# Moving the layout transfers of q and k to later places in a four-batch attention and mixer kernel

## The chip, the cores and the metric

The kernel runs on one core of a Trainium2 chip. Its time is device microseconds (us) of one launch; for each kernel three executions are shown by their median and their ends. One more execution was profiled, and every row below is from that one.

## The reference

Batch 4, 8 heads, 768 positions, head width 64. The attention works in chunks of 32 queries; each chunk sees 8 memory keys, the 16 positions before it, its own 32 and the 8 after it. Its result x then goes through a low-rank token mix and a two-layer network:

```python
for c in range(24):
    k_full = concat([mem_k, k[l_start:r_end]]); v_full = concat([mem_v, v[l_start:r_end]])
    a = softmax(q_c @ k_full.T / 8)
    out[c] = a @ v_full
x = out.transpose(0, 2, 1, 3).reshape(4, 768, 512)
u = x + ((x.transpose(0, 2, 1) @ U) @ V).transpose(0, 2, 1)     # U 768x32, V 32x768
y = u + relu(u @ w_ch1) @ w_ch2                                  # 512 -> 2048 -> 512
```

U, V, w_ch1 and w_ch2 arrive as float64; q, k, v and the memory as float32.

## The kernel before

**Arithmetic.** The float64 weights are decoded on the device; each becomes a high and a low half (`w1h`, `w1l`, cast on ACT at L387, subtracted on DVE at L391), and each product of the network is made in three passes of 128-row matmuls. DRAM scratch (`w1s`, `w1x`) keeps low halves and sums of weights for the later batches.

**Order of the batches.** Batch 0 runs its attention, then 32 *units* (`both_blocks`). A unit is one hidden group f of 128 columns for one half of the 768 positions: `w1_step` (12 matmuls at L1475), a split into `hh` (ACT) and `hl` (DVE), and `w2_step` for the unit before. The first 20 units decode the weights as they go; units 20 to 25 are f = 10 to 15 of the first half, units 26 to 31 of the second. The attention of batch 1 is a Python generator, and a table, `PLACE`, says after which matmuls of units 18 to 31 it is advanced by how many pieces.

Batches 1 to 3 (`sevens`) make pairs of hidden groups with seven products of sums (`six`, L1302), with weights that a ring (`wlo`, four items ahead) brings from the scratch (L1261, L465 to L468). Batch 1 differs: its first part makes ten single hidden groups f = 0 to 9 (`half_of`, `other`), with sums of weights made on ACT and DVE (L488, L489) and stored to the scratch (L494). While batch b runs, the attention of batch b + 1 is advanced by `give()`, which spreads 49 pieces evenly over a batch's places. The *second part* of a batch is the loop over n = 0 to 15, which only needs kept hidden groups.

**Layout of q and k.** For batches 0 and 1, q and k are loaded as rows (`kraw`, L539 to L549), regrouped (`kn`; POOL at L567 for batch 1), turned by TensorE (L618) and copied by ACT into `kall` (L655 to L659) and `qt` (L679). For batches 2 and 3 a DRAM-to-DRAM transfer first rearranges them: `spread(b)` issues eight transfers on SP's queue, four for k and then four for q, each of 3072 rows of 128 bytes (L172). Then `load_blocks` (L526) reads 256 KB at a time and DVE transposes blocks of 32x32 into `kall` (L637, two instructions per load) and `qt` (L668, one). The table `SPREAD` says in which unit of batch 0 a spread is issued: one in each of units 2 to 17.

**What sets the order.** PE and SP keep the order in which the program is written. From unit 27 on (and on ACT and POOL after the first units) a scheduler orders ACT, DVE and POOL by priority. SP issues almost all DMAs, in order: an issue that must wait for its data holds back all behind it.

```python
for n, (blk, f, where, begins, ends) in enumerate(units):
    ...
    for _ in range(SPREAD.get(n, 0)):
        next(spreading)
    ...
    hid_ = w1_step(0, blk, f, w1l, between if n else joins)
```

Of the kernel before, what the change touches and what calls it, by code (L numbers as in the profile page):

```python
# [48 lines left out]
LATER = 4  # L49
NPIECE = 49  # L50
DIRECT = 2
SPREAD = {n: 1 for n in range(2, 18)}
PLACE = {
# [7 lines left out]
def chunk_attn_then_mixer_kernel(  # L61
# [454 lines left out]
    def attention(b, xs):  # L516
# [114 lines left out]
        def k_blocks(T, h):  # L631
            raw, p = kn.pop((T, h)), slice(2 * h, 2 * h + 2)
            kt = kall[:, NB * (T % 2):NB * (T % 2) + NB, p]
            other = kall[:, NB * ((T + 1) % 2) + NB - 1, p]
            at, own = NM + LEFT, NM + LEFT + CK
            for q_ in range(2):
                nc.vector.transpose(out=kt[:, :, q_, at:own], in_=raw[:, q_])  # L637
            nc.scalar.copy(out=kt[:, 1:, :, NM:at], in_=kt[:, 0:NB - 1, :, own - LEFT:own])
            nc.scalar.copy(out=kt[:, 0:NB - 1, :, own:], in_=kt[:, 1:, :, at:at + NW - own])
            if T > 0:  # L640
                nc.scalar.copy(out=kt[:, 0, :, NM:at], in_=other[:, :, own - LEFT:own])
                nc.scalar.copy(out=other[:, :, own:], in_=kt[:, 0, :, at:at + NW - own])
# [648 lines left out]
    def sevens(b, give, following, last_step=None):  # L1291
# [45 lines left out]
        if few:  # L1337
            banks, lows = {}, {}

            def half_of(f):  # L1340
                banks[f], lows[f] = hidden_bank(), next_item()
                six(banks[f], w1h[f][:, 0:2], lows[f][:, 0], 0, True)
                keep(kept(f), banks[f])

            def other(f):
                low = lows.pop(f)
                six(banks[f], w1h[f][:, 2:4], low[:, 1], 1, False)
                if f < few - 2:
                    take_value(f, low.rearrange("p i c n -> p (i c) n"), work_home)
                return split(banks.pop(f)[:, :TOK])  # L1350

            last_step()
            half_of(0)
            half_of(1)
            for _ in gen[0]:
                pass
            gen[0] = attention(b + 1, xs)
            prev = (0, 0, True, None) + other(0)
            for f in range(1, few):
                h = other(f)  # L1360
                if f == 1:
                    send()
                if f + 3 == few:
                    plain.close()
                    su1 = ctx.enter_context(tc.tile_pool(name="su1", bufs=1, reuse_waits="tile"))
                    hst.append(su1.tile([P, 4, TOK], F32, name="hst2"))
                    seven["pools"] = su1, []
                if f + 1 == few:
                    closing.enter_context(tc.manual_schedule(engines=CLOSING))
                early, late = NEXTS.get(few - f, (0, 0))  # L1370
                for _ in range(early):
                    next(coming[0])
                give()
                if f + 1 < few:
                    half_of(f + 1)
                w2_step(b, 0, *prev, give)
                for _ in range(late):
                    next(coming[0])
                if f + 2 == few:
                    save_sums()  # L1380
                prev = (f, 0, False, None) + h
            held_w.close()
            seven["pools"][1].append(ctx.enter_context(tc.tile_pool(name="su2", bufs=1, side="right", reuse_waits="tile")))
# [63 lines left out]
        for n, f in enumerate(order):  # L1447
            hid_ = split(kept(f))
            if n == 0:
                rows.pop()  # L1450
            if n == 2:
                save_sums()
                send()
            if n == LATER and following is not None:
                following()
            give()
            if n + 2 < few:
                other_half(left[n + 2])
                if n < LATER:
                    give()  # L1460
            if prev is not None:
                w2_step(b, 1, *prev)
            prev = (f, 0, n == 0, True if n == NF - 1 else None) + hid_
# [159 lines left out]
    front[0] = False  # L1623
    wide[0] = None

    gen, coming = [None], [iter(())]

    def pace(slots):
        tried, given = [0], [0]

        def give():
            tried[0] += 1
            if tried[0] > slots:
                next(coming[0], None)
                return
            while given[0] < NPIECE * tried[0] // slots:
                next(gen[0], None)
                given[0] += 1

        return give  # L1640
# [12 lines left out]
    last_step = both_blocks()  # L1653
    for b in range(1, B):
        slots = 2 * 2 * NPL - 1 + 6 * (NF // 2 - NPL) + 2 + 2 * LATER if b == 1 else 6 * (NF // 2) + LATER
        if b > 1:
            gen[0] = attention(b + 1, xs) if b + 1 < B else iter(())
            coming[0] = seven_u(b + 1) if b + 1 < B else iter(())
        sevens(b, pace(slots), following_batch(b) if b + 1 < B else None, last_step)
        for _ in coming[0]:  # L1660
            pass
    manual.close()
# [29 lines left out]
```

## Time and profile before

| | |
|---|---|
| three executions: median (ends) | 667.92 us (666.58 to 668.73) |
| the profiled execution: time / span | 667.71 us / 665.8 us |
| PE busy | 629.6 us, 95% of the span |
| DVE / ACT / POOL busy | 365.4 / 236.1 / 77.5 us |
| DMA | 115.02 MB in 168704 packets, of them 100956 under 512 B |

PE is TensorE's matmuls, PEld its weight loads; the two overlap. A time in brackets at the end of a row of the timeline is the idle time of that engine just before, with what ended it. SPq is SP's queue of DMA issues. PEclk is the granted TensorE clock as a share of full speed (1.00 is 2.4 GHz, 0.50 is 1.2 GHz). In this execution batch 0's attention lasts to about 55 us, its units to about 232 us, batch 1 to 388 us, batch 2 to 537 us.

### The profile page before, as it was taken

How to read it: one execution, taken by the hardware profiler on the slowest of the kernel's cores; microseconds unless marked ns; L12 is line 12 of the kernel's file. 1: busy time of each engine (PE TensorE's matmuls, PEld its weight loads, DVE VectorE, ACT ScalarE, POOL GpSimd, SP SyncE). 2: the span in 40 equal slices, each digit the busy share in tenths (PEclk: the TensorE clock that was granted, in tenths of full speed). 3: DMA queues.
4: the chain of work that ended last, by engine and by line, in shares of the span. 5: the costliest groups of instructions: out<-in, count | busy, mean ns of one | idle time of the engine just before them, and what ended most of it. 6: DMA issues, size and time to landing. Idle time of an engine off the chain costs nothing.

```text
span 665.8 us, 14969 instructions
## 1 busy us (share of the span) xinstructions
PE 629.6 (95%) x6078; PEld 544.2 (82%) x6078; DVE 365.4 (55%) x715; ACT 236.1 (35%) x557; POOL 77.5 (12%) x106
## 2 busy tenths in 40 slices
PE   7688999986899999999999999999999999999997
PEld 4547999975687788889879888889988899999886
DVE  5947788893667556953734744434536732222322
ACT  4525435344533445532312622413224512121221
POOL 5100000004136546200400000000000000000000
PEclk9989999997999999999999999999999999999999
DMA  8796999999477279766573059685523046555301
GB/s 233 152 322 214 237 226 241 230 241 300 116 137 214 96 268 264 260 171 155 167 233 104 28 166 264 205 230 136 159 64 126 1 129 190 157 156 161 109 1 47
DMA packets 168704, 115.02 MB, mean 173 GB/s; under 512 B 100956, under 2 KB 139484, under 8 KB 168636
## 3 DMA queue, kind: packets, MB, share of 16 engines
q1 hardware_dynamic: 168012, 113.92, 61.3%
q8 instruction: 48, 0.79, 0.5%
q10 hardware_dynamic: 624, 0.15, 0.1%
q14 instruction: 20, 0.16, 0.1%
HBM read 90.83 MB, written 28.97 MB: 180 GB/s over the span
## 4 chain that ended last, share of the span: by engine, by line
PE 59%; DVE 4%; DMA 4%; SPq 3%; issue 1%; ACT 1%; POOL 1%; ACTq 0%
PE ps_h L1302 23%; PE acc L1526 17%; PE acc L1536 9%; DMA blocks<-spread 3%; PE ps_a L773 2%; PE acc L1520 2%; PE ps_h L1475 2%; PE ps_a L699 1%; SPq L600 1%; PE ps_a L1198 1%; DMA w1l<-w1s 1%; PE ps_a L803 1%; PE ps_a L753 1%; DVE x L1491 1%; PE ps_a L1103 1%
## 5 line engine op out<-in xcount | busy, mean ns | idle before, releaser
L1526 PE MATMUL acc<-w,hh 128*128 128x512 f32 x612 | 158.5, 395 | 0.6 <-ACT hh L1316 0.6
L1526 PEld LDWEIGHTS acc<-w,hh 128*128 128x128 f32 x612 | 112.9, 188 | 20.7 <-ACT hh L1316 0.9
L1536 PE MATMUL acc<-w,hl 128*128 128x512 f32 x306 | 87.9, 396 | 0.0
L1536 PEld LDWEIGHTS acc<-w,hl 128*128 128x128 f32 x306 | 57.3, 189 | 11.9
L1302 PE MATMUL ps_h<-t12h,w1l 128*128 128x384 f32 x192 | 56.3, 345 | 2.0 <-DMA w1l<-w1s 1.4
L1302 PE MATMUL ps_h<-bh,w1l 128*128 128x384 f32 x192 | 52.9, 340 | 0.0
L1302 PE MATMUL ps_h<-t34h,w1l 128*128 128x384 f32 x152 | 46.5, 347 | 1.0 <-issue 0.8
L1475 PE MATMUL ps_h<-uh,w1h 128*128 128x384 f32 x124 | 43.0, 350 | 2.2 <-ACT w1h L387 1.2
L1475 PE MATMUL ps_h<-ul,w1h 128*128 128x384 f32 x124 | 41.6, 339 | 0.4 <-DVE ul L1180 0.4
L1302 PEld LDWEIGHTS ps_h<-t12h,w1l 128*128 128x128 f32 x192 | 35.3, 188 | 5.3 <-ACT hh L1316 2.5
L1317 DVE SCALAR_TENSOR_TENSOR hl<-ps_h,hh 128x384 fp32r<-128x384 f32 x29 | 16.1, 555 | 42.8 <-ACT hh L1316 42.7
L1324 DVE TENSOR_TENSOR c<-ps_h,c 128x384 f32<-128x384 f32 x19 | 10.5, 553 | 50.2 <-PE ps_h L1302 50.2
L1316 ACT ACTIVATE hh<-hst 128x384 fp32r<-128x384 f32 x36 | 18.9, 525 | 49.9 <-PE acc L1526 44.6
L1317 DVE SCALAR_TENSOR_TENSOR hl<-hst,hh 128x384 fp32r<-128x384 f32 x36 | 20.1, 557 | 29.0 <-PE acc L1536 28.5
L1302 PEld LDWEIGHTS ps_h<-bh,w1l 128*128 128x128 f32 x192 | 35.1, 188 | 0.8
L1302 PE MATMUL ps_h<-b,w1l 128*128 128x384 f32 x174 | 35.4, 339 | 0.1
L1324 DVE TENSOR_TENSOR hst<-ps_h,hst 128x384 f32<-128x384 f32 x36 | 19.9, 553 | 24.4 <-ACT hst L1328 15.3
L1302 PE MATMUL ps_h<-t12l,w1l 128*128 128x384 f32 x96 | 32.4, 338 | 0.0
L1316 ACT ACTIVATE hh<-ps_h 128x384 fp32r<-128x384 f32 x29 | 14.2, 490 | 49.1 <-PE ps_h L1302 49.0
L1302 PEld LDWEIGHTS ps_h<-b,w1l 128*128 128x128 f32 x174 | 30.9, 188 | 0.5 <-DVE hst L1324 0.5
L1302 PEld LDWEIGHTS ps_h<-t34h,w1l 128*128 128x128 f32 x152 | 28.0, 188 | 3.1 <-issue 1.7
L1328 ACT COPY c<-ps_h 128x384 f32<-128x384 f32 x19 | 9.1, 479 | 59.5 <-PE ps_h L1302 59.5
(250 smaller groups left out, 1201.9 us busy)
## 6 DMA issues: line engine op xcount, KB each, us to landing
w1l<-w1s SPq DMA_DIRECT2D x155, 256.0 KB
rw<-in_moe_w_ch_dram SPq DMA_DIRECT2D x14, 512.0 KB
out_dram<-x SPq DMA_DIRECT2D x24, 256.0 KB
blocks<-spread SPq DMA_DIRECT2D x24, 256.0 KB
vb<-in_v_dram SPq DMA_DIRECT2D x56, 98.0 KB
raw<-in_moe_w_ch_dram SPq DMA_DIRECT2D x20, 256.0 KB
rw<-in_moe_w_ch_dram SPq DMA_DIRECT2D x16, 256.0 KB
w1s<-sums SPq DMA_DIRECT2D x16, 256.0 KB
```

What stands on the lines that cost most here:

```text
L600: nc.sync.dma_start(out=vt[r0:r0 + NW - NM, n0:n1, D * j:D * j + D], in_=bass.AP(rows.tensor, rows.offset, [[step, count], [CK * step, n1 ...
L699: nc.tensor.matmul(out=psv[s][(slice(CK * i, CK * i + CK), t) + ((p // 2, p % 2) if b >= DIRECT else (p % 2, p // 2))], lhsT=qt[p // 2][ro ...
L773: nc.tensor.matmul(out=psv[g][CK * i:CK * i + CK, t, j], lhsT=pt[s][rows, 2 * t + k_, CK * i:CK * i + CK], rhs=vt[rows, NI * t + i, D * j: ...
L1302: nc.tensor.matmul(out=ps[:, :TOK], lhsT=w_, rhs=u, start=(start and m == 0), stop=(m == 5), skip_group_check=True,)
L1316: nc.scalar.activation(out=hh, in_=c, func=AF.Relu)
L1317: nc.vector.scalar_tensor_tensor(out=hl, in0=c, scalar=0.0, in1=hh.bitcast(F32), op0=ALU.max, op1=ALU.subtract,)
L1324: nc.vector.tensor_tensor(out=out, in0=ps[:, :TOK], in1=in1, op=ALU.add)
L1328: nc.scalar.copy(out=out, in_=ps[:, :TOK])
L1475: nc.tensor.matmul(out=ph[:, :TOK], lhsT=w[:, c, :], rhs=u[c], start=(m == 0), stop=(m + 1 == len(parts)),)
L1520: nc.tensor.matmul(out=acc[tt], lhsT=h[:, sl], rhs=w, start=False, stop=(m == 2))
L1526: nc.tensor.matmul(out=acc[tt], lhsT=h[:, sl], rhs=w, start=(begins and m == 0), stop=False,)
L1536: nc.tensor.matmul(out=acc[tt], lhsT=hl[:, sl], rhs=w2h[f], start=False, stop=ends is not None)
```

## The change

The 16 spreads leave units 2 to 17. Batch 2's four k spreads go to units 22 to 25. Two of its q spreads go right behind batch 0's last step, at the start of batch 1, and two more into batch 1's step f = 1, just ahead of the loads of batch 2's first blocks. Batch 3's eight spreads go one each to n = 4 to 11 of batch 1's second part. There, at n = 12 and 14, the generator of batch 3's attention is also advanced by two pieces each time: the memory values and the four block loads of its first third are then issued before batch 2 starts; `pace` starts batch 2 with those 4 pieces counted as given, so that the later ones keep their places. In `k_blocks` one DVE transpose of 128x512 elements takes the place of two of 128x256.

```diff
--- before.py
+++ after.py
@@ -49,7 +49,7 @@
 LATER = 4
 NPIECE = 49
 DIRECT = 2
-SPREAD = {n: 1 for n in range(2, 18)}
+SPREAD = {22: 1, 23: 1, 24: 1, 25: 1}
 PLACE = {
     18: [0, 0, 0, 1], 19: [0, 0, 0, 2], 20: [0, 0, 0, 3], 21: [3, 3, 4, 5], 22: [6, 7, 9, 11], 23: [12, 13, 14, 15],
     24: [15, 15, 16, 17], 25: [18, 18, 19, 20], 26: [20, 20, 21, 22], 27: [22, 23, 24, 24], 28: [25, 25, 26, 26],
@@ -633,8 +633,7 @@
             kt = kall[:, NB * (T % 2):NB * (T % 2) + NB, p]
             other = kall[:, NB * ((T + 1) % 2) + NB - 1, p]
             at, own = NM + LEFT, NM + LEFT + CK
-            for q_ in range(2):
-                nc.vector.transpose(out=kt[:, :, q_, at:own], in_=raw[:, q_])
+            nc.vector.transpose(out=kt[:, :, :, at:own].rearrange("c i p n -> c p i n"), in_=raw)
             nc.scalar.copy(out=kt[:, 1:, :, NM:at], in_=kt[:, 0:NB - 1, :, own - LEFT:own])
             nc.scalar.copy(out=kt[:, 0:NB - 1, :, own:], in_=kt[:, 1:, :, at:at + NW - own])
             if T > 0:
@@ -1350,6 +1349,8 @@
                 return split(banks.pop(f)[:, :TOK])
 
             last_step()
+            for _ in range(2):
+                next(spreading)
             half_of(0)
             half_of(1)
             for _ in gen[0]:
@@ -1367,6 +1368,9 @@
                     seven["pools"] = su1, []
                 if f + 1 == few:
                     closing.enter_context(tc.manual_schedule(engines=CLOSING))
+                if f == 1:
+                    for _ in range(2):
+                        next(spreading)
                 early, late = NEXTS.get(few - f, (0, 0))
                 for _ in range(early):
                     next(coming[0])
@@ -1451,8 +1455,13 @@
             if n == 2:
                 save_sums()
                 send()
+            if few and LATER <= n < LATER + 8:
+                next(spreading)
             if n == LATER and following is not None:
                 following()
+            if few and n in (LATER + 8, LATER + 10):
+                for _ in range(2):
+                    next(upcoming[0])
             give()
             if n + 2 < few:
                 other_half(left[n + 2])
@@ -1623,10 +1632,10 @@
     front[0] = False
     wide[0] = None
 
-    gen, coming = [None], [iter(())]
-
-    def pace(slots):
-        tried, given = [0], [0]
+    gen, coming, upcoming = [None], [iter(())], [None]
+
+    def pace(slots, ahead):
+        tried, given = [0], [ahead]
 
         def give():
             tried[0] += 1
@@ -1653,10 +1662,12 @@
     last_step = both_blocks()
     for b in range(1, B):
         slots = 2 * 2 * NPL - 1 + 6 * (NF // 2 - NPL) + 2 + 2 * LATER if b == 1 else 6 * (NF // 2) + LATER
-        if b > 1:
-            gen[0] = attention(b + 1, xs) if b + 1 < B else iter(())
+        if b == 1:
+            upcoming[0] = attention(3, xs)
+        else:
+            gen[0] = upcoming[0] if b + 1 < B else iter(())
             coming[0] = seven_u(b + 1) if b + 1 < B else iter(())
-        sevens(b, pace(slots), following_batch(b) if b + 1 < B else None, last_step)
+        sevens(b, pace(slots, 4 if b == 2 else 0), following_batch(b) if b + 1 < B else None, last_step)
         for _ in coming[0]:
             pass
     manual.close()
```

Lines move by -1 up to about L1340, then by +9 to +11 (L1475 becomes L1484, L1317 becomes L1316). PE's order does not change. Three other places do.

First, SP's queue at batch 1's first loads of k (`kraw`), in unit 17 before. These are the rows before, with the last spread of the sixteen, and then the rows now.

```order
L334 DMA rw_1752<-in_moe_w_ch_dram 128x2x256
L334 DMA raw<-in_moe_w_ch_dram 128x2x256
L351 DMA raw<-in_moe_w_ch_dram 128x512 x2
L172 DMA spread_1634<-in_q_dram 3072x1x32
L366 DMA w1s_131<-w1h_1741 128x2x256
L366 DMA w1s_131<-w1l 128x2x256
L539 DMA kraw<-in_k_dram 120x4x128
L540 DMA kraw<-in_k_dram 8x4x128
```

```order
L334 DMA rw_1733<-in_moe_w_ch_dram 128x2x256
L334 DMA raw<-in_moe_w_ch_dram 128x2x256
L351 DMA raw<-in_moe_w_ch_dram 128x512 x2
L366 DMA w1s_131<-w1h_1722 128x2x256
L366 DMA w1s_131<-w1l 128x2x256
L539 DMA kraw<-in_k_dram 120x4x128
L540 DMA kraw<-in_k_dram 8x4x128
```

The spread ahead of `kraw` is gone, as are the fifteen further up the queue; the first one now stands behind all `kraw` and `qraw` loads of batch 1.

Second, ACT during batch 1's turning of q and k: copies out of PSUM into `kall` and `qt`, between casts of the last weights (L387) and decoding steps (L230). Before:

```order
L659 COPY kall<-ps_a 128x2x2x12
L679 COPY qt<-ps_a 128x2x128 x4
L655 COPY kall<-ps_a 128x2x8x16
L656 COPY kall<-ps_a 128x2x7x12
L655 COPY kall<-ps_a 128x2x8x16
L656 COPY kall<-ps_a 128x2x7x12
L659 COPY kall<-ps_a 128x2x2x12
L387 CAST w1h_2065<-vb_115 128x512
L387 CAST w2last<-vb_115 128x512
L230 ACTIVATE vb_115<-rw_1752 128x256
L230 ACTIVATE vb_115<-raw 128x256 x3
L679 COPY qt<-ps_a 128x2x128 x4
```

and now:

```order
L678 COPY qt<-ps_a 128x2x128 x4
L654 COPY kall<-ps_a 128x2x8x16
L655 COPY kall<-ps_a 128x2x7x12
L654 COPY kall<-ps_a 128x2x8x16
L655 COPY kall<-ps_a 128x2x7x12
L658 COPY kall<-ps_a 128x2x2x12
...
L658 COPY kall<-ps_a 128x2x2x12
L678 COPY qt<-ps_a 128x2x128 x2
L387 CAST w1h_2047<-vb_115 128x512
L387 CAST w2last<-vb_115 128x512
L230 ACTIVATE vb_115<-rw_1733 128x256
L678 COPY qt<-ps_a 128x2x128 x2
L230 ACTIVATE vb_115<-raw 128x256 x3
```

The first four `qt` copies now stand ahead of both groups of five `kall` copies, and two of the last four ahead of the casts and the decoding.

Third, SP's queue in batch 1's steps f = 0 and 1, where batch 2's first blocks are loaded (`mv` are memory values, `w1l` ring items, `w1s` stores). Before:

```order
L494 DMA w1s_132<-vb_115 128x512 x2
L494 DMA w1s_132<-sums 128x512 x2
L1501 DMA out_dram<-x 128x512 x3
L956 DMA mv<-in_mem_v_dram 8x4x64 x2
L526 DMA blocks<-spread_1121 128x2x256
L468 DMA w1l<-w1s_129 128x2x256
L526 DMA blocks<-spread_1121 128x2x256
L526 DMA blocks<-spread_1293 128x2x256
```

and now:

```order
L494 DMA w1s_132<-vb_115 128x512 x2
L494 DMA w1s_132<-sums 128x512 x2
L1510 DMA out_dram<-x 128x512 x3
L172 DMA spread_3101<-in_q_dram 3072x1x32 x2
L955 DMA mv<-in_mem_v_dram 8x4x64 x2
L526 DMA blocks<-spread_2011 128x2x256
L468 DMA w1l<-w1s_129 128x2x256
L526 DMA blocks<-spread_2011 128x2x256
L526 DMA blocks<-spread_3101 128x2x256
```

Two spreads of q now stand ahead of all block loads, and the load from `spread_3101` reads what they write.

## Rows read from the trace of the kernel before

**Rows 1.** The page's first part: busy time of each engine, share of the span, instructions.

```profile
PE 629.6 (95%) x6078; PEld 544.2 (82%) x6078; DVE 365.4 (55%) x715; ACT 236.1 (35%) x557; POOL 77.5 (12%) x106
```

**Rows 2.** Timeline of PE, 146 to 184 us: start, length, instruction, idle before.

```profile
154.61 1.11 PE L618 MATMUL ps_a<-ident,kn 128*128 128x128 f32 x4 [7.32 <-POOL kn L567]
...
164.35 0.63 PE L618 MATMUL ps_a<-ident,kn 128*128 128x128 f32 x4 [1.30 <-ACT kall L659]
...
169.66 1.47 PE L699 MATMUL ps_a<-kall,qt 64*32 64x64 f32 x126 [1.84 <-ACT qt L679]
...
183.14 0.44 PE L1475 MATMUL ps_h<-uh,w1h 128*128 128x384 f32 x1 [1.15 <-ACT w1h L387]
```

**Rows 3.** Timeline of POOL at 153 us, columns as in rows 2.

```profile
153.94 0.61 POOL L567 COPY kn<-kraw 128x512 f32<-128x512 f32 x1 [130.74 <-DMA kraw<-in_k_dram]
```

**Rows 4.** Timeline of SP, 145 to 151 us.

```profile
145.45 0.55 SPq L172 DMA_DIRECT2D spread<-in_q_dram  x1
146.10 3.28 SPq L366 DMA_DIRECT2D w1s<-w1h  x1
149.99 0.46 SPq L539 DMA_DIRECT2D kraw<-in_k_dram  x1
```

**Rows 5.** Timeline of DVE at 128 us.

```profile
128.47 0.69 DVE L391 TENSOR_TENSOR w1l<-vb,w1h 128x512 fp32r<-128x512 f32 x1
```

**Rows 6.** Busy time by stretches: columns stand in the first line.

```profile
core 0: us, PE busy (x) PEld busy (x) DVE busy (x) ACT busy (x) POOL busy (x), PEclk, DMA share, GB/s
53.00:147.00 94.00, 91.98 (x464) 82.75 (x463) 80.85 (x140) 44.32 (x97) 0.00 (x0) 1.00 0.93 225
57.00:59.00 2.00, 1.39 (x8) 1.07 (x7) 1.62 (x3) 0.59 (x2) 0.00 (x0) 1.00 0.91 148
```

**Rows 7.** Busy time by stretches around the long idle time of PE.

```profile
147.30:151.80 4.50, 0.00 (x0) 0.00 (x0) 2.84 (x5) 0.00 (x0) 0.00 (x0) 1.00 1.15 273
151.80:154.60 2.80, 0.00 (x0) 0.00 (x0) 0.00 (x0) 0.00 (x0) 0.61 (x1) 0.50 1.07 285
154.60:158.60 4.00, 3.99 (x14) 3.60 (x15) 0.00 (x0) 1.87 (x8) 2.23 (x4) 0.50 1.01 309
```

**Rows 8.** Timeline of PE, batch 2's first steps.

```profile
398.45 1.65 PE L1526 MATMUL acc<-w,hh 128*128 128x512 f32 x6 [0.61 <-ACT hh L1316]
...
415.80 0.41 PE L1302 MATMUL ps_h<-t12h,w1l 128*128 128x384 f32 x1 [1.39 <-DMA w1l<-w1s]
...
421.43 0.62 PE L1302 MATMUL ps_h<-t34h,w1l 128*128 128x384 f32 x2 [0.84 <-issue]
```

**Rows 9.** Busy time by stretches where the spreads go, columns as in rows 6.

```profile
170.00:190.00 20.00, 18.35 (x442) 15.61 (x425) 15.14 (x29) 9.31 (x26) 0.56 (x1) 1.00 0.36 102
220.00:240.00 20.00, 19.49 (x99) 16.37 (x98) 14.80 (x24) 10.22 (x22) 7.99 (x7) 1.00 0.39 140
240.00:270.00 30.00, 29.75 (x275) 26.69 (x274) 17.05 (x38) 15.03 (x44) 17.34 (x19) 1.00 0.95 300
348.00:388.00 40.00, 40.00 (x200) 34.53 (x199) 22.87 (x46) 15.81 (x30) 0.00 (x0) 1.00 0.22 63
```

**Rows 10.** Timelines of SP, DVE and ACT at batch 2's first blocks.

```profile
241.42 0.39 SPq L526 DMA_DIRECT2D blocks<-spread  x1
...
244.34 0.77 DVE L637 STREAM_TRANSPOSE kall<-blocks 128x256 f32<-128x256 f32 x2 [1.83 <-DMA blocks<-spread]
...
247.49 0.55 DVE L1317 SCALAR_TENSOR_TENSOR hl<-ps_h,hh 128x384 fp32r<-128x384 f32 x1
...
251.63 0.56 DVE L1317 SCALAR_TENSOR_TENSOR hl<-ps_h,hh 128x384 fp32r<-128x384 f32 x1
...
250.17 0.41 ACT L488 CAST vb<-vb 128x256 fp32r<-128x256 f32 x1 [2.18 <-DMA w1s<-vb]
```

**Rows 11.** Groups of DVE by line and shape: busy, mean ns, idle before.

```profile
L637 DVE STREAM_TRANSPOSE kall<-blocks 128x256 f32<-128x256 f32 x24 | 9.1, 419 | 8.9 <-DMA blocks<-spread 8.9
L668 DVE STREAM_TRANSPOSE qt<-blocks 128x512 f32<-128x512 f32 x12 | 8.1, 692 | 1.4 <-DMA blocks<-spread 1.4
```

## The prediction, made before the changed kernel ran

> **What bounds the kernel now.** I read first the page's busy times: PE is busy 629.6 us of 665.8 [rows 1], so the kernel is a chain of matmuls, and a change that leaves PE's order alone can only move PE's 36 us of idle time and its clock. So the second view is PE's timeline, searched for idle times, and the third the timelines of whatever ended them. One idle time stands out, 7.32 us before 154.61, in the unit where batch 1's first k is turned [rows 2]. It was ended by a POOL copy, which had itself waited 130.74 us for the load of `kraw` [rows 3]. That load was issued late: SP issued the last spread at 145.45, needed 3.28 us for the store behind it, and reached `kraw` only at 149.99 [rows 4]. Nothing that SP issues there is bound to come so late: the low half that the neighbouring stores read was being made at 128.47 [rows 5]. What held the queue is the traffic. From 53 to 147 us the DMA engines are 0.93 busy [rows 6], with the sixteen spreads among it. Two smaller idle times, 1.30 and 1.84 us, follow in the turning, ended by ACT's copies [rows 2]. And the idle time costs once more: the clock, 1.00 before, is 0.50 from 151.8 to 158.6 [rows 7].
>
> **The change part by part.** All terms are against the profiled execution, 667.71 us, which is 0.2 us under the median of the runs shown, 667.92.
>
> **A, the spreads leave units 2 to 17.** What a spread costs isn't shown by itself. The two microseconds from 57 to 59, with spreads under way, moved 148 GB/s at a share of 0.91 [rows 6], so 163 GB/s at full use; a spread of 3072 x 128 bytes, 393 kB, is then about 2.4 us of all engines, and sixteen are 38 us of DMA out of 94. PE gains nothing from that in the units themselves (91.98 of 94 us busy [rows 6]); what it gains is SP's lead. Without the spreads `kraw` can go out from about 130 us, when the low half is there [rows 5], instead of 149.99: 20 us earlier, against an idle time of 7.32. I take all of it: **-7.3 us**. Bounds: a lead of 15 us, after the loads around it, would do as well, and less than 7 would leave a part; nothing in the rows asks for so little.
>
> **B, the clock.** After the idle time PE worked 3.99 us at 0.50 [rows 7]. At full clock the same work takes half: **-2.0 us**. If the idle time goes, so does this. The Trainium skill's page "TensorE: Matmul & The Clock Gate", section "Terms", puts the penalty at the throttled time times (1 - K/N); that is 6.8 us times 0.5, or 3.4, and the sum would be 1.4 lower. The rows speak against it here: PE stood idle in 2.8 of the 6.8 us [rows 7], where a clock costs nothing.
>
> **C, ACT's copies.** The `qt` copies of the first third now precede ten `kall` copies, and two of the last four precede the decoding, so the waits of 1.30 and 1.84 us [rows 2] lose their cause as far as it was ACT's order. Bounds: 0 and -3.1, with a little more if the wait of 1.15 us for the cast of `w1h` at 183.14 [rows 2] goes too. As both waits stand right behind the long one, in work pressed together by it, I take three quarters: **-2.3 us**.
>
> **D, batch 3's first loads before batch 2.** In batch 2's first steps PE waits 0.61, 1.39 and 0.84 us [rows 8]: for ACT's `hh`, for a ring item, and without a named cause. Loads that are already there take a burst of six issues out of that time. Bounds 0 and -2.8; I take the two that a late queue explains best, the last two: **-2.2 us**.
>
> **E, the new wait at batch 1's start.** Two q spreads now stand on SP directly ahead of batch 2's first loads, and the load of q's blocks must wait until all four q spreads have landed. Behind it in the queue are ring items and the next stores. Before, the first block load went out at 241.42 [rows 10]. Two spreads are 4.8 us of all engines, and from 240 to 270 us these are 0.95 busy [rows 9], so the delay isn't soaked up; with the 3.28 us that an issue behind a spread took [rows 4], SP is up to 8.1 us late. What is late next: DVE's turning at 244.34, the `hl` behind it on DVE at 251.63, and on ACT the cast at 250.17, which waited 2.18 us for a store [rows 10] and has the next `hh` behind it. PE's step is 4.14 us long there (247.49 to 251.63, from `hl` to `hl` [rows 10]), and the ring is four items ahead, so of 8.1 us at least 4.1 are covered, and the k blocks, which need only the queue, come before the q blocks. Bounds 0 and +8.1; nearer to the covered end, as the block loads feed work that is due a batch later: **+1.5 us**. Against this stands a rule of the Trainium skill, page "DMA: Bandwidth & Descriptors", section "Two DMAs through the same engine are not ordered": a DMA that reads what another wrote must wait on its completion semaphore, being behind it in the queue isn't enough; and its section "Anatomy of one DMA — SWDGE (gpsimd) path" has a fixed cost of about 2 us, mostly completion. By it the q blocks are later by 2 us more, and the sum would be 657.4; no row here shows that wait by itself.
>
> **F, edits that I cost at nothing.** The single transpose saves 2 x 419 - 692 = 146 ns, twelve times, 1.75 us of DVE [rows 11]. DVE is busy 365.4 of 665.8 us [rows 1], and the transposes serve a batch that is not yet due; if DVE were the last in line before `hl`, 0.15 us each would show. The four k spreads need 9.7 us of DMA where 0.64 of 20 us is free (170 to 190); the first two q spreads 4.8 where 12 of 20 is free (220 to 240); batch 3's eight spreads and four blocks (256 KB, under 1 us each at 300 GB/s) about 23 where 31 of 40 is free, 348 to 388 [rows 9]. That free time is the cover; without it, each spread would hold SP's queue for some 2.4 us.
>
> **Sum:** -7.3 - 2.0 - 2.3 - 2.2 + 1.5 = -12.3, so 667.7 - 12.3 = **655.4 us**. A measurement of this kernel can tell about 0.3%, 2.0 us, from no change.
>
> **The rivals.**
> 1. *The new wait is not covered* (E at its upper bound): SP's lag of 8.1 us reaches PE through DVE's or ACT's queue. For it: the share of 0.95 [rows 9]. Against: the four items of the ring, and loads that are due late. 655.4 + 6.6 = **662.0 us**, up to 664 if C fails besides. Chance 0.13.
> 2. *The stall is replaced by the next wait*: with `kraw` early, PE runs into ACT's copies, and the waits of 1.30 and 1.84 [rows 2] double instead of going: +3.1 in place of -2.3, **660.8 us**. For it: ACT's copies have ended both. Against: ACT is busy only 44.32 of 94 us before [rows 6]. Chance 0.08.
> 3. *It doesn't do what it says*: batch 3's early loads find their buffers in use, and SP waits for them at the end of batch 1 as it did in batch 2. D is then nothing: **657.6 us**. Chance 0.12.
> 4. *Slower*: the lag on SP is never made up between 240 and 280 us, so that each of three pairs of stores (`w1s`) comes late, ACT's cast stands in front of `hh` each time, and PE loses 8.1 - 4.1 = 4.0 us, enough to bring the clock to 0.50, with 2.0 more for the work after it [rows 7]. One such loss is 6.0; without E the sum is 653.9, so two make 665.9, no change, and it is slower from the third on: 653.9 + 18 = **671.9 us**. For it: 0.95 in rows 9. Against: the first pair of q spreads goes into 220 to 240 us, where only 0.39 is in use [rows 9], and the whole kernel moves no more bytes than before. Chance 0.05.
>
> **How the numbers follow.** The forecast as worked out, within some 3 us, has 0.62. The range: below, all of C and D, the 1.15 us and no E give 667.7 - 7.3 - 2.0 - 3.1 - 2.8 - 1.2 = 651.3, and runs lie up to 1.3 us under their median; so 650. Above, A and B alone with E at 5 give 667.7 - 9.3 + 5 = 663.4; so 663.5, with rivals 2, 3 and most of 1 inside. Outside are rival 4, the worst of rival 1, and a gain that I don't see. Faster by over 2.0 us: the forecast and rivals 1 to 3, less the part of them that meets unseen costs: 0.90. Within: 0.05. Slower: 0.05, rival 4.
>
> **What would show it.** Right: in the changed profile `kraw` is issued at 130 to 140 us; PE has no idle time over 2 us from 140 to 175; the clock stays 1.00 there; PE's total idle time falls by about 10 us; the block loads at batch 1's start go out some 5 us later than 241.42 but no `hl` or `hh` there ends a PE wait over 1 us; batch 2's first steps have waits under 1 us in sum. Wrong: a PE wait of over 2 us between 232 and 280 us, ended by DVE, ACT or a ring item (rival 1 or 4); waits of over 2 us ended by ACT in the turning (rival 2); block loads of batch 3 issued only after 388 us less the gain (rival 3).

## The result and the profile after

The changed kernel takes 656.42 us (median of 4, 655.92 to 658.14), the kernel before 667.25 beside it (4, 666.36 to 668.73): a ratio of 0.984, interval 0.9813 to 0.9867. That is 10.8 us faster; the forecast was 655.4 us, 12.3 under the profiled execution. The total is near, in part by luck: from the start of batch 0's units on, the forecast's terms came to 9.1 us and not 12.3, and 1.9 us of scatter ahead of the units lies between the two profiled executions. The profiled execution of the changed kernel took 656.56 us, its span 654.7. The page's first part, to set against [rows 1]:

```profile
PE 626.5 (96%) x6075; PEld 543.0 (83%) x6078; DVE 366.7 (56%) x703; ACT 235.6 (36%) x557; POOL 80.0 (12%) x106
```

PE's idle time fell from 36 to 28 us, its busy time by 3. Where: this is SP's timeline at batch 1's first k, and PE's there and on to 176 us (start, length, instruction, idle before), then the busy time of both stretches (columns as in [rows 6]).

```profile
126.63 0.38 SPq L366 DMA_DIRECT2D w1s<-w1h  x1
127.35 0.38 SPq L366 DMA_DIRECT2D w1s<-w1l  x1
127.82 0.46 SPq L539 DMA_DIRECT2D kraw<-in_k_dram  x1
```

```profile
145.91 0.63 PE L618 MATMUL ps_a<-ident,kn 128*128 128x128 f32 x4 [0.46 <-DVE x L1500]
...
169.43 0.44 PE L1484 MATMUL ps_h<-uh,w1h 128*128 128x384 f32 x1 [1.15 <-ACT w1h L387]
```

```profile
53.00:147.00 94.00, 91.78 (x464) 82.94 (x465) 82.19 (x138) 42.93 (x95) 6.56 (x8) 1.00 0.61 197
...
145.40:158.60 13.20, 12.43 (x198) 11.11 (x198) 10.77 (x18) 10.61 (x38) 4.96 (x6) 1.00 0.81 188
```

`kraw` is issued at 127.82 instead of 149.99 [rows 4], the first of the two stores ahead of it takes 0.38 us instead of 3.28, the wait of 7.32 us [rows 2] is 0.46, ended by another releaser, and the clock stays at 1.00. Between 145.91 and 169.43 PE has no wait of 0.4 us or more: the two waits for ACT are gone whole. But 100 us later there are three new ones, on PE's timeline:

```profile
257.04 0.66 PE L1197 MATMUL ps_a<-ident,x 128*128 128x128 f32 x4 [1.97 <-ACT uc L1199]
...
261.58 0.65 PE L752 MATMUL ps_a<-ident,pt 128*128 128x128 f32 x4 [1.43 <-ACT pt L724]
...
269.99 0.75 PE L772 MATMUL ps_a<-vb,pT 64*32 64x64 f32 x53 [1.63 <-ACT pT L755]
```

PE's order is the same in both kernels, so the lead of the changed one can be read at matching matmuls: start before less start after.

| matmul | before | after | lead |
|---|---|---|---|
| first of batch 0's units | 59.45 | 57.60 | 1.9 |
| batch 1's first turn of k (L618) | 154.61 | 145.91 | 8.7 |
| the turn that waited 1.30 | 164.35 | 152.28 | 12.1 |
| first scores of batch 1 (L699) | 169.66 | 155.93 | 13.7 |
| batch 1, first part (L1302) | 257.24 | 243.10 | 14.1 |
| batch 1, a value product (L773) | 279.50 | 269.99 | 9.5 |
| batch 1, products (L1302) | 317.08 | 306.89 | 10.2 |
| batch 2, a ring item (L1302) | 415.80 | 403.94 | 11.9 |
| six us on | 420.26 | 409.56 | 10.7 |
| end of the span | 665.8 | 654.7 | 11.1 |

Three things to explain: what set the k load's time, why 4.6 us were lost again in batch 1, and 1.9 us of lead before the first moved instruction (the first spread was at 53 us, after the lead had arisen).

### The profile page after: what moved, and what is told of

It is laid out like the page before. It is cut to its first block, busy times and chain, and to the rows that moved or that the text cites. A ratio compares the mean times of both kernels' runs of the same rounds, so it can differ in the third digit from the quotient of the medians.

```text
span 654.7 us, 14949 instructions
## 1 busy us (share of the span) xinstructions
PE 626.5 (96%) x6075; PEld 543.0 (83%) x6078; DVE 366.7 (56%) x703; ACT 235.6 (36%) x557; POOL 80.0 (12%) x106
## 4 chain that ended last, share of the span: by engine, by line
PE 60%; DMA 5%; DVE 5%; POOL 1%; issue 1%; SPq 1%; ACT 1%; ACTq 0%
PE ps_h L1301 23%; PE acc L1535 18%; PE acc L1545 9%; PE ps_a L772 2%; PE acc L1529 2%; PE ps_h L1484 2%; DMA blocks<-spread 1%; PE ps_a L698 1%; DMA spread<-in_q_dram 1%; DMA w1l<-w1s 1%; PE ps_a L1197 1%; PE ps_a L802 1%; PE ps_a L752 1%; DMA w1s<-vb 1%; DMA vb<-mv 1%
## 5 line engine op out<-in xcount | busy, mean ns | idle before, releaser
L1545 PEld LDWEIGHTS acc<-w,hl 128*128 128x128 f32 x306 | 56.8, 188 | 11.9
L1484 PE MATMUL ps_h<-uh,w1h 128*128 128x384 f32 x124 | 42.5, 347 | 2.2 <-ACT w1h L387 1.2
L1484 PE MATMUL ps_h<-ul,w1h 128*128 128x384 f32 x124 | 41.3, 337 | 0.4 <-DVE ul L1179 0.4
L1316 DVE SCALAR_TENSOR_TENSOR hl<-ps_h,hh 128x384 fp32r<-128x384 f32 x29 | 16.0, 553 | 45.7 <-ACT hh L1315 45.6
L1316 DVE SCALAR_TENSOR_TENSOR hl<-hst,hh 128x384 fp32r<-128x384 f32 x36 | 20.0, 557 | 29.0 <-PE acc L1545 28.6
```

The source lines that it names most:

```text
L1316: nc.vector.scalar_tensor_tensor(out=hl, in0=c, scalar=0.0, in1=hh.bitcast(F32), op0=ALU.max, op1=ALU.subtract,)
L1484: nc.tensor.matmul(out=ph[:, :TOK], lhsT=w[:, c, :], rhs=u[c], start=(m == 0), stop=(m + 1 == len(parts)),)
L1545: nc.tensor.matmul(out=acc[tt], lhsT=hl[:, sl], rhs=w2h[f], start=False, stop=ends is not None)
```

## The experiments

All kernels but one were timed in five rounds beside the kernel before, in three groups on three chips; each ratio is to the kernel before of its own group.

**Which spreads hold the k load.** Three kernels leave everything as before but the table:

```diff
-SPREAD = {n: 1 for n in range(2, 18)}
+SPREAD = {**{n: 1 for n in range(2, 12)}, **{n: 1 for n in range(22, 28)}}    # last six later
+SPREAD = {**{n: 1 for n in range(8, 18)}, **{n: 1 for n in range(22, 28)}}    # first six later
+SPREAD = {**{n: 1 for n in range(2, 16)}, **{n: 1 for n in range(22, 24)}}    # last pair later
```

The last six:

> The kernel before, with six of its sixteen spreads (the ones of units 12 to 17) moved to units 22 to 27, behind batch 1's loads of k and q; nothing else of the change. Theory: the stall of 7.3 us, the half clock after it and the two waits for ACT go with these six alone (6 x 2.4 = 14.4 us of DMA ahead of the k load): 667.3 - 11.6 = 655.7 us, and batch 1's first part loses nothing. Rival: SP's lead needs all sixteen out of the way; then a stall of several us is left: 658 to 664 us. Second rival: ACT's two waits of 1.30 and 1.84 us don't go with the stall: 658.8 us.

Measured: 655.08 us (654.5 to 656.05), ratio 0.9827 (0.9803 to 0.9851). The theory holds: with six spreads moved the clock's fall, ACT's waits and all but 0.72 us of the stall are gone. Only its last part fails: batch 1's first part does lose time, as is read below. The first six, the last pair, and the kernel before once more:

> The kernel before, with the spreads of units 2 to 7 gone and six put into units 22 to 27, so that units 8 to 17 keep one each, up to the k load; nothing else of the change, and ACT's copies keep the order of before. Theory (the lag of SP adds up over all units: a store behind a spread takes 4.4 us of SP there and 0.37 without): ten spreads leave a lag of some 13 us in place of 21, the k load goes out at about 142 us, the stall is under 1 us and the half clock is gone; ACT's two waits, 1.30 and 1.84 us, came from the stall and go with it: 655 to 657.5 us. Rival (only the spreads just ahead of the k load matter, since earlier lag is made up): the stall and the half clock stay whole, 665 us or more. Second rival (the two waits came from ACT's order, which is not changed here): the stall goes, the waits stay, 658 to 660.5 us.

> The kernel before, with only the last two of the sixteen spreads (units 16 and 17) moved, to units 22 and 23; ACT's copies keep the order of before. Theory (each spread ahead of the k load costs SP what the store behind it is held, 3.3 to 4.7 us): two are 8 us, about the whole stall of 7.3; under 1 us of it is left, the clock stays at 1.00 and the time is 655 to 658 us. Rival (a spread costs its 2.4 us of DMA): 4.8 us of the stall go, 2.5 are left: 660 us. Second rival (the lag of all sixteen adds up, 21 us over 16, 1.3 each): 4.7 us of the stall are left, with the half clock: 664 us.

> The kernel before, once more with a profile, to see what in its profile repeats. Theory: the stall of about 7 us at batch 1's first k, the half clock and ACT's two waits come again; the start of batch 0's units, which the first profile had at 59.45 us and five kernels with the same order up to there had at 55.6 to 58.0, is scatter and comes out nearer to 57. Rival: it is 59 us again, and so something in the changed kernels speeds up batch 0's attention, 2 us that no step of the forecast has.

Measured: 662.17 us (658.31 to 664.78), ratio 0.9942 (0.9917 to 0.9967); 660.73 us (656.57 to 665.25), ratio 0.9921 (0.9892 to 0.9949); and 666.02 us for one execution of the kernel before, beside a median of 665.49. PE's timelines, the kernel before again, the first six later, the last pair later:

```profile
152.33 1.12 PE L618 MATMUL ps_a<-ident,kn 128*128 128x128 f32 x4 [8.13 <-POOL kn L567]
162.58 0.63 PE L618 MATMUL ps_a<-ident,kn 128*128 128x128 f32 x4 [1.30 <-ACT kall L659]
167.89 1.47 PE L699 MATMUL ps_a<-kall,qt 64*32 64x64 f32 x126 [1.84 <-ACT qt L679]
```

```profile
147.79 0.66 PE L618 MATMUL ps_a<-ident,kn 128*128 128x128 f32 x4 [3.37 <-POOL kn L567]
157.26 0.63 PE L618 MATMUL ps_a<-ident,kn 128*128 128x128 f32 x4 [1.30 <-ACT kall L659]
162.84 1.62 PE L699 MATMUL ps_a<-kall,qt 64*32 64x64 f32 x126 [1.91 <-ACT qt L679]
```

```profile
146.50 0.66 PE L618 MATMUL ps_a<-ident,kn 128*128 128x128 f32 x4 [1.55 <-POOL kn L567]
156.40 0.63 PE L618 MATMUL ps_a<-ident,kn 128*128 128x128 f32 x4 [1.30 <-ACT kall L659]
161.76 1.92 PE L699 MATMUL ps_a<-kall,qt 64*32 64x64 f32 x126 [1.90 <-ACT qt L679]
```

The stall is not an accident of one execution, and its size follows the k load. Issue of `kraw` on SP, less the start of the first unit in the same trace:

| kernel | `kraw` | first unit | difference | stall |
|---|---|---|---|---|
| before | 149.99 | 59.45 | 90.5 | 7.32 |
| before again | 147.79 | 56.37 | 91.4 | 8.13 |
| first six later | 143.10 | 56.57 | 86.5 | 3.37 |
| last pair later | 140.63 | 57.11 | 83.5 | 1.55 |
| last six later | 125.96 | 55.60 | 70.4 | 0.72, from DVE |
| last eight later (below) | 127.52 | 57.29 | 70.2 | 0.37, from DVE |
| the change, all sixteen | 127.82 | 57.60 | 70.2 | 0.46, from DVE |

Against the mean of the two first, 91.0, the first six are worth 4.5 us or 0.7 each, the last two 7.5 or 3.7 each, the last six 20.6; ten more add nothing. So part of an early lag is made up, and of a late one none; both the theory of a lag that adds up evenly and its rival were too simple. Each late spread costs about what the store behind it is held [rows 4], not its 2.4 us of DMA. So the last pair's theory had the right cost; but 1.55 us of stall stayed where it had under 1, the clock fell, and the time is 2.7 us above its range. The floor of 70 us is the data of the two stores ahead of `kraw`: in the changed kernel the cast of `w1h` ends at 126.60 and its store is issued at 126.63, `w1l` is made at 127.33 and its store is issued at 127.35. An issue of `kraw` ahead of them was not tried.

Two more things are read here. The waits for ACT, 1.30 and 1.84 to 1.91 us, stand unchanged in both kernels with a small stall: these have ACT's order of before, while the kernel with the last six moved has the changed order and neither wait. The waits go with that order, whatever the stall. And in both of these profiles the clock falls after the shorter stall as well. Busy time by stretches, first six later, then last pair later:

```profile
144.40:147.80 3.40, 0.03 (x2) 0.01 (x1) 2.87 (x5) 0.00 (x0) 0.88 (x1) 1.00 1.01 284
147.80:151.10 3.30, 3.30 (x14) 2.90 (x15) 0.00 (x0) 1.67 (x8) 1.84 (x3) 0.59 0.96 288
```

```profile
144.95:146.50 1.55, 0.00 (x1) 0.00 (x1) 1.55 (x4) 0.00 (x0) 0.61 (x1) 1.00 1.07 268
...
148.40:152.30 3.90, 3.90 (x17) 3.81 (x16) 1.77 (x3) 2.18 (x7) 2.65 (x4) 0.57 0.84 251
...
161.90:165.60 3.70, 3.70 (x133) 3.50 (x126) 1.63 (x5) 0.93 (x5) 0.00 (x0) 0.54 0.69 147
```

With the last pair moved, the clock is down twice, after 1.55 us of idle time and after the 1.90 us of ACT's wait, for 3.9 and 3.7 us of busy PE at 0.57 and 0.54. That is some 3.4 us, worked out as busy time times one less the clock (3.9 x 0.43 + 3.7 x 0.46), more than the 2 us that the kernel before loses to it in the first profile. By the medians these two kernels gained 3.3 and 4.8 us, where the stall shrank by 4.0 to 4.8 and by 5.8 to 6.6. The profiled execution of the last pair, 664.67 us, is the second slowest of its twelve, so its two falls of the clock need not be the rule. Nor does the length of a wait alone decide: later in the same profile PE waits 2.73 us, and the clock stays at 1.00.

```profile
268.81 0.66 PE L753 MATMUL ps_a<-ident,pt 128*128 128x128 f32 x4 [2.73 <-ACT pt L725]
```

```profile
269.00:273.00 4.00, 4.00 (x26) 3.63 (x26) 4.00 (x10) 3.48 (x10) 1.48 (x2) 1.00 0.64 230
```

**What was lost in batch 1.** The changed kernel with batch 2's q spreads elsewhere:

```diff
-SPREAD = {22: 1, 23: 1, 24: 1, 25: 1}
+SPREAD = {n: 1 for n in range(22, 30)}    # all four q spreads in units
+SPREAD = {n: 1 for n in range(2, 10)}     # batch 2's eight early, as before
+SPREAD = {n: 1 for n in range(22, 28)}    # two q spreads in units, the pair at f == 1 stays
             last_step()
-            for _ in range(2):
-                next(spreading)
...
-                if f == 1:
-                    for _ in range(2):
-                        next(spreading)
```

> Batch 2's four q spreads go to units 26 to 29 of batch 0, behind its k spreads, instead of to batch 1's steps; all else is as in the changed kernel. Theory: in the changed kernel PE loses 4.2 us between 243 and 270 us (its lead over the kernel before falls from 14.1 to 9.5 us, then settles near 10), because two q spreads stand on SP ahead of batch 2's first blocks and make DVE, POOL and ACT late by 3 to 5 us. Without them that loss goes: 656.4 - 4.2 = 652.2 us, no PE wait over 1 us from 240 to 275. Rival: the loss comes from the total of DMA traffic there (share 0.99 from 226 to 256), which the two spreads are only 4.8 of 30 us of: under 1.5 us gained, 655 to 656.4. Second rival: the four more spreads in units 26 to 29 hold up the stores and weights of the units' end and cost as much there as is gained: 656 to 660.

> Batch 2's eight spreads go to units 2 to 9 (where the kernel before had them), batch 3's eight to the places that the changed kernel gives them; no spreads in units 22 to 29 or in batch 1's first part. Theory: eight spreads less (some 19 us of DMA) are enough for SP to be early at batch 1's first k, so the 11.6 us of the stall, the clock and ACT's copies go in full, as do the 4.2 us lost in batch 1: 652.2 us. Rival: what made the k load late was not the spreads' sum but each one's place on SP, or the weights' traffic itself; then with eight left part of the stall is left, 2 us or more of it, and the time is 655 us or more.

Measured: 653.93 us (652.9 to 654.79), ratio 0.9809 (0.9785 to 0.9834); and 652.59 us (651.75 to 652.86), ratio 0.9788 (0.9765 to 0.9811). In the first kernel no PE wait over 0.7 us is left between 226 and 290 us, but there is a new one of 1.26 us before 220.28, ended by DVE, and its lead falls from 13.2 to 11.3 between 199 and 221 us: theory and second rival both hold in part, and 2.5 of 4.2 us are gained. The second kernel has neither loss. The chain is best seen by setting the two side by side. SP, DVE, POOL and ACT of the changed kernel:

```profile
226.62 3.25 SPq L172 DMA_DIRECT2D spread<-in_q_dram  x2
229.92 2.27 SPq L955 DMA_DIRECT2D mv<-in_mem_v_dram  x2
232.24 0.39 SPq L526 DMA_DIRECT2D blocks<-spread  x1
...
233.18 1.13 SPq L526 DMA_DIRECT2D blocks<-spread  x2
```

```profile
235.56 0.71 DVE L636 STREAM_TRANSPOSE kall<-blocks 128x512 f32<-128x512 f32 x1 [2.61 <-DMA blocks<-spread]
236.19 0.72 DVE L489 TENSOR_TENSOR sums<-vb,sums 128x256 fp32r<-128x256 f32 x2
```

```profile
236.99 1.31 POOL L475 TENSOR_TENSOR vb<-w1h,w1l 128x512 f32<-128x512 f32 x1 [5.67 <-DMA blocks<-spread]
...
252.91 3.16 POOL L485 TENSOR_TENSOR vb<-vb 128x256 f32<-128x256 f32 x4
```

```profile
255.29 0.41 ACT L488 CAST sums<-vb 128x256 fp32r<-128x256 f32 x1 [2.63 <-POOL vb L485]
256.10 0.40 ACT L488 CAST sums<-vb 128x256 fp32r<-128x256 f32 x1 [0.40 <-POOL vb L485]
256.41 0.58 ACT L1199 COPY uc<-ps_a 128x512 f32<-128x512 f32 x1
```

and of the one with eight early spreads:

```profile
226.85 1.08 SPq L955 DMA_DIRECT2D mv<-in_mem_v_dram  x2
227.98 0.39 SPq L526 DMA_DIRECT2D blocks<-spread  x1
```

```profile
233.24 0.71 DVE L636 STREAM_TRANSPOSE kall<-blocks 128x512 f32<-128x512 f32 x1 [1.40 <-DMA blocks<-spread]
233.88 0.38 DVE L489 TENSOR_TENSOR sums<-vb,sums 128x256 fp32r<-128x256 f32 x1
```

```profile
234.34 1.30 POOL L475 TENSOR_TENSOR vb<-w1h,w1l 128x512 f32<-128x512 f32 x1 [2.81 <-DMA blocks<-spread]
...
248.08 3.17 POOL L485 TENSOR_TENSOR vb<-vb 128x256 f32<-128x256 f32 x4
```

```profile
250.47 0.41 ACT L488 CAST sums<-vb 128x256 fp32r<-128x256 f32 x1 [0.62 <-POOL vb L485]
```

The first block load is 4.3 us later, held by two spreads and a slow `mv` behind them. DVE's subtractions for the sums of weights (L489) stand in DVE's queue behind its transpose of a block, and POOL's next sum (L475) starts 0.08 us after they end in both kernels, at 236.91 and at 234.26; the rows put POOL's wait of 5.67 (2.81) down to a block load, but it is this DVE instruction that ended last. From there POOL stays late, by 2.7 us first and by 4.8 at its last sums (L485). ACT's cast waits 2.63 for those instead of 0.62, and in ACT's queue behind that cast stands the copy `uc`, for which PE waits 1.97. Which pair of q spreads does it:

> The changed kernel with the first two q spreads of batch 2 in units 26 and 27 instead of behind batch 0's last step; the two at f = 1, directly ahead of batch 2's first block loads, stay. Theory: the pair at f = 1 is the whole cost of some 4 to 5 us between 250 and 275 us, since SP was idle behind the first pair in the changed kernel (first pair at 209 us, SP with nothing to issue from 215 to 221.7): no change against the changed kernel run beside it, within 1 us, and PE's waits of 1.4 to 2.5 us between 250 and 275 us stay. Rival: both pairs share the cost: 2 us or more faster than the changed kernel.

> The changed kernel, a second time, beside the three others of this call. Theory: the loss between 250 and 275 us comes again, three waits of PE of 1.4 to 2.5 us that sum to about 5, and the time is 656 to 657 us. Rival: the loss is scatter of one execution: waits under 1 us there and a time that is the one of the kernel with eight spreads early.

> The kernel with batch 2's eight spreads in units 2 to 9 and the rest of the change, a second time, beside the changed kernel on one chip. Theory: 3 to 5 us faster than the changed kernel, its loss in batch 1. Rival: the difference between the two was one between chips, under 1.5 us.

Measured, in one group: two q spreads in units 657.14 us (655.39 to 661.48), ratio 0.9843 (0.9807 to 0.9878); the changed kernel again 656.96 (653.1 to 661.78), 0.9831 (0.9785 to 0.9876); eight early again 655.28 (652.51 to 657.29), 0.9803 (0.977 to 0.9837). Moving the first pair changes nothing, and PE's two waits stay, here in its own timeline:

```profile
257.80 1.01 PE L1197 MATMUL ps_a<-ident,x 128*128 128x128 f32 x4 [2.48 <-ACT uc L1199]
270.74 1.17 PE L772 MATMUL ps_a<-vb,pT 64*32 64x64 f32 x96 [1.69 <-ACT pT L755]
```

The pair at f = 1 is what the cost goes with. The lead at two matmuls of batch 1 (257.24 and 290.02 us in the kernel before) shows it over all profiles: the five of kernels with that pair lose 4.7 to 5.9 us between the two, the eight others at most 2.4. The changed kernel again has PE's waits at 2.69 and 1.69 us, and there the clock falls after both, which it did after none of the three in the first profile:

```profile
257.51 0.66 PE L1197 MATMUL ps_a<-ident,x 128*128 128x128 f32 x4 [2.69 <-ACT uc L1199]
```

```profile
257.50:262.00 4.50, 4.49 (x16) 3.95 (x17) 4.50 (x10) 3.91 (x9) 1.47 (x2) 0.62 0.94 333
...
272.00:275.40 3.40, 3.40 (x11) 2.96 (x10) 2.81 (x8) 0.65 (x2) 0.00 (x0) 0.50 0.25 65
```

The pair costs 4.7 us of lead in the first of these profiles and 5.8 in the second, where some 3.4 us of busy time are the clock's (4.49 x 0.38 + 3.40 x 0.50) and the wait of 1.43 is gone. By spans less the start of the units, eight early spreads are 4.4 us (597.1 to 592.7) and 5.4 us (599.8 to 594.4) shorter than the change; the medians of this last group, 1.7 apart with intervals that overlap, can't show as much; those of the first two groups, 3.8 apart, have intervals that just miss each other. And the kernels with the last six or the last pair later also have waits of 2.2 and 2.7 us there, before 259.58 and 268.81, without any spread in batch 1: something else makes this place tight as well, and what it is stays open.

**Early loads, and the one-pass turn.** Without the former (`upcoming` is not advanced, `pace` starts at 0), without the latter (two transposes again), and without both, moving batch 3's eight spreads alone:

```diff
-SPREAD = {n: 1 for n in range(2, 18)}
+SPREAD = {n: 1 for n in range(2, 10)}
...
+            if few and LATER <= n < LATER + 8:
+                next(spreading)
             if n == LATER and following is not None:
```

> As the changed kernel, but batch 3's attention isn't begun in batch 1: its memory values and first four block loads come in batch 2 at the places that they had in the kernel before. Theory: PE's lead grew from 9.6 to 11.1 us in batch 2's first steps, so these early loads are worth 1.5 us: 656.4 + 1.5 = 657.9 us, with the waits of 0.6 and 1.4 us of batch 2's start back. Rival: that lead came from the spreads' new places, and early loads are worth nothing: 656.4 us.

> The changed kernel with k turned by two DVE instructions of 128x256 again; all else as changed. Theory: 1.75 us of DVE more, off the path: 656.4 us, no difference that can be measured. Rival: in batch 1's first part, where DVE's transposes wait for block loads and the sums behind them set POOL and ACT, 0.15 us each and another order of the scheduler show: 657 to 659 us.

> The kernel before, with batch 2's eight spreads left in units 2 to 9 and batch 3's eight at n = 4 to 11 of batch 1's second part; no early loads and two transposes for each k load, as before. Theory: this one move carries the whole of the stall, the half clock and ACT's waits, and costs nothing in batch 1; against the kernel with eight spreads early and all the rest of the change (652.6 us) only the early loads are missing, 1.1 us: 653.7 us. Rival: the early loads or the one-pass transpose carry more than that: over 655 us.

Measured: 657.53 us (655.72 to 661.64), ratio 0.9873 (0.9843 to 0.9903); 657.33 us (655.84 to 658.85), ratio 0.9863 (0.9829 to 0.9896); 653.87 us (652.86 to 656.49), ratio 0.9792 (0.9761 to 0.9823). Neither part can be told from nothing beside the change's own interval; 657.33 us lies in the range of the one-pass turn's theory as well as of its rival. The last edit, on the kernel before, is as good as the best found: 3.1 us under the change in the same group, though the intervals overlap.

## Why the prediction was right, and where it wasn't

- **A, -7.3: right.** The wait of 7.32 us is 0.46, -6.9; `kraw` went out when the low half's store did, as the step said. Its price was not what carried it: a late spread is worth 3.7 us of SP and an early one 0.7, and six would have been enough for the wait.
- **B, -2.0: right.** From the turn of k to the next wait the lead grew by 3.4 us, of which 1.3 is that wait: 2.1 for the clock. The rule of the Trainium skill's page "TensorE: Matmul & The Clock Gate", section "Terms", which gives 3.4 us, counts idle time as well, and the row decides against it. What the step didn't see: the clock is not lost in proportion to the stall. In the one profile with 1.55 us of stall left it was lost all the same.
- **C, -2.3: the mechanism was right, the term too small.** All 3.1 us went. The step took three quarters because both waits stood behind the long one "in work pressed together by it"; the kernels with a short stall and the old order show that this played no part.
- **D, -2.2: too large, and none of it told from scatter.** The three waits of [rows 8], 2.8 us, became four, of 0.20, 0.16 and these two:

```profile
403.94 0.41 PE L1301 MATMUL ps_h<-t12h,w1l 128*128 128x384 f32 x1 [0.39 <-DMA w1l<-w1s]
...
409.56 0.34 PE L1301 MATMUL ps_h<-t34l,w1l 128*128 128x384 f32 x1 [0.98 <-issue]
```

1.7 us, so -1.1 in waits; the lead grew from 10.2 to 11.8 there, lost 1.1 again at a new wait of 1.24 us without a named cause (437.32), and ended at 11.1, so -0.9. But the second profile of the changed kernel waits 2.9 us at the same place (0.51, 0.93 and 1.46), and the kernel before waits 1.8 in its second. The later two of the changed kernel's second profile:

```profile
400.43 1.31 PE L1301 MATMUL ps_h<-b,w1l 128*128 128x384 f32 x6 [0.93 <-DVE hst L1323]
...
411.81 0.34 PE L1301 MATMUL ps_h<-t34l,w1l 128*128 128x384 f32 x1 [1.46 <-issue]
```

Over all profiles PE idles 1.3 to 3.0 us there in the seven with early loads and 1.8 to 3.4 in the seven without. Without them the median was only 1.1 us more, and the span the same 654.7. The step read one execution's waits as the kernel's. Rival 3, that these loads would be held for buffers, did not come: they were issued at 364.90, before batch 2.
- **E, +1.5: mis-sized.** The lead fell from 14.1 to 9.5 us and came back to 10.2: +3.9. The step saw SP's lag, the cast on ACT and what stands behind it, but covered the lag by the ring and by loads "due a batch later". For PE the ring did cover what it feeds: none of its waits there is for a ring item. The sums of weights, which pass through DVE and POOL to ACT in the order of their queues, were not in the step. This is rival 1's mechanism at about half of its price. Its sign, a PE wait of over 2 us between 232 and 280 us, is just missed in this profile (1.97) and there in the four others with the pair (2.3 to 2.7). The wait that the step took from the Trainium skill's page "DMA: Bandwidth & Descriptors", section "Two DMAs through the same engine are not ordered", is there, but it is 0.2 us and not 2: SP held the first load of q's blocks, issued at 233.95, for a spread. In SP's waits from 232.7 to 235 us:

```profile
SPq L526 <- DMA spread<-in_q_dram: 0.2, 1, 0.2
```

The 2 us were the Trainium skill's figure for transfers that gpsimd issues; these are issued by SP. What cost was the queue, held 3.25 us by the two issues and 2.27 by the next.
- **F, 0: not contradicted.** The single transpose takes 699 ns instead of 2 x 419 [rows 11], a saving of 0.14 us each:

```profile
L636 DVE STREAM_TRANSPOSE kall<-blocks 128x512 f32<-128x512 f32 x12 | 8.3, 699 | 8.1 <-DMA blocks<-spread 8.1
```

- **Not in the sum:** the 1.9 us before the units. Eleven further profiles of kernels with the same order up to there have the first unit between 55.6 and 59.4 us, the kernel before itself at 59.45 and 56.37. It is scatter between executions; between the two profiles it happened to favour the changed kernel.

So from the units on the terms are -6.9 - 2.1 - 3.1 + 3.9 - 0.9 = -9.1, where -12.3 was forecast: D and E were too good by 3.7 together, C too cautious by 0.8, A and B near. With the 1.9 of scatter that is 11.0, and the spans differ by 11.1; that this comes so near to 12.3 is in part luck. That the medians too differ by 10.8 and, in the last group, 11.3 (668.3 less 656.96) is more than 9.1; the 2 us between stay open, with one or two profiles of each kernel against scatter of 3 us at the start.

## What to carry to other kernels

Look for the first load that a queue issues too late, and move away what stands just ahead of it on that queue: here the last two of sixteen transfers made the load 7.5 us late, the first six 4.5. Put them where the queue has nothing urgent behind them, not only where the DMA engines are free: a pair ahead of block loads that nobody needed soon cost 4 us, through a transpose, sums of weights and a cast in the engines' own queues. A stall cut to a fifth still cost its clock in the one profile taken of it. And read a place with waits of a microsecond in more than one execution before giving them a price.

## What the runs showed of the hardware

A DRAM-to-DRAM transfer of 3072 rows of 128 bytes holds its queue longer than its own issue shows: 0.55 us for the issue [rows 4], then 3.3 to 4.8 us for a store right behind it, against 0.37 to 0.38 where no spread stands ahead. With several in a row the time shows in the issues themselves. This is SP's timeline of the changed kernel at batch 3's q spreads:

```profile
354.58 7.89 SPq L172 DMA_DIRECT2D spread<-in_q_dram  x4
362.51 2.34 SPq L955 DMA_DIRECT2D mv<-in_mem_v_dram  x2
364.90 2.72 SPq L526 DMA_DIRECT2D blocks<-spread  x4
```

Four issues took 7.89 us, 2 us each, the same order as the estimate of 2.4 us for one transfer. TensorE's granted clock fell after an idle time of 1.55 us and after one of 1.90 in one profile (to 0.57 and 0.54 over the stretches shown), and stayed at 1.00 after one of 2.73 in the same; in the two profiles of the changed kernel it stayed after 1.97 and fell after 2.69 and 1.69. What decides it, no run here shows.
